# Fewer switches of the TensorE array in a head pair: regrouped full-array work, split score units and a hand order for VectorE

## The chip, the core and the metric

The kernel runs on one core of one Trainium2 chip. The metric is the device time of one execution in microseconds; the kernel before took 359.49 us (median of 3 runs, 359.22 to 360.35). Five engines work side by side, each through its own list of instructions in order: TensorE (PE; its weight loads are shown as PEld), VectorE (DVE), ScalarE (ACT), GpSimd (POOL) and SyncE (SP, which here only issues transfers). They wait for each other with semaphores. TensorE writes to PSUM[...]; VectorE and ScalarE read it.

## The reference

Two stages. Attention, for 4 batches and 8 heads of 768 positions and 64 features: keys are cut into 24 chunks of 32; each query takes the 6 chunks with the highest upper bound of its score and attends to them causally. Then a switch layer: every token goes to the one of 8 experts with the highest logit and comes back scaled by the gate.

```python
k_min, k_max = chunk minimum and maximum of k         # 24 chunks of 32 keys
ub = sum(max(q * k_min, q * k_max), features)         # upper bound per query and chunk
top_chunks = argsort(where(causal, ub, -1e9))[..., -6:]
mask = selected(top_chunks) & (pos_q >= pos_k)
attn = softmax(where(mask, (q @ k.T) / sqrt(64), -1e9)) @ v
x = attn as rows of tokens, 3072 x 512
logits = x @ w_gate; e = argmax(logits)
out = gate * (relu(x @ w1[e]) @ w2[e])                # 512 -> 1024 -> 512
```

## The kernel before: the parts concerned

A head pair is two heads of one batch, so there are 16 pairs, `i` = 0 to 15 (`b`, `hp` = batch and pair in it). The loop is pipelined over pairs: while pair `i` attends, pair `i+1` selects its chunks, pair `i+2` transposes its keys and queries, and pairs `i-1` and `i-2` turn their output into token rows. The expert stage follows the 16 pairs.

The scores of a pair are cut into 7 units of (up to) 128 keys x 384 queries x 2 heads. Each unit has a product into PSUM (`ps`), an exponential on ScalarE (`P`), a causal cut of diagonal blocks on GpSimd, a product with v into `po`, and an addition on VectorE into `acc` for the sums of the softmax. Units 0 and 1 make the output of the first 384 queries, 2 to 6 that of the others. The chosen chunks reach the scores as extra rows of the operands (`QSB` rows from 64 on, from `nsel`).

The pools, whose numbers of buffers matter:

```python
ps_m = tc.alloc_tile_pool(name="ps_m", bufs=3, space=PSUM)   # transposes, bounds, routing
ps_s = tc.alloc_tile_pool(name="ps_s", bufs=2, space=PSUM)   # scores
ps_o = tc.alloc_tile_pool(name="ps_o", bufs=1, space=PSUM)   # attention output "po"
...
ot = work.tile([128, 384], FP32, tag="ot", bufs=3)           # output, copied from po
```

Preparation of a pair (the full array is used by the transposes of 128 columns; `ub` has two 64-column halves; `mask` transposes 64 columns):

```python
def k_half(hf):                      # steps k0, k1
    ... nc.tensor.transpose(pt, k tile) x3
    nc.vector.tensor_reduce(kmx, pk, max); nc.vector.tensor_reduce(kmn, pk, min)
    nc.scalar.activation(kte[0:64, 0, ...], pt[0:64]); nc.scalar.activation(kte[0:64, 1, ...], pt[64:128])
def q_t(hf):  ... nc.tensor.transpose(pt, q tile) x3              # q0, q1
def q_e(hf):  # q0e, q1e: VectorE copies qT, ScalarE makes qA = |q| and QSB; GpSimd copies QSB later
def kse():    # VectorE, for each head: KS = kmx + kmn, KD = kmx - kmn (4 operations)
def ub():     # TensorE: KS.T @ qT + KD.T @ qA; ScalarE copies it to ubT
def select(): # TensorE transposes ubT x3; VectorE: + bias, top 8 of 24 (12 operations), nsel = below the 6th
def mask():   # TensorE transposes nsel x6; ScalarE copies both heads to QSB
```

Scores and output:

```python
def scores(i, u):
    ps = ps_s.tile([128, 2, 512], FP32, tag="s")
    for n, (kb, w, c0) in enumerate(parts):        # units 1 and 6 have two parts, 256 and 128 queries
        for hd in range(2):
            nc.tensor.matmul(pv[:, hd, :], lhsT=kte[:, hd, ts(kb, 128)], rhs=qsb[...])
    for pv, (kb, w, c0) in zip(pvs, parts):
        nc.scalar.activation(P[:, :, ds(c0, w)], pv, AF.Exp)        # one for each part
    ...                                                             # causal cut on GpSimd
def attend(i, u):
    if first: s["po"] = ps_o.tile([128, 384], FP32, tag="o")
    ... nc.tensor.matmul(po[64 * hd:64 * hd + 64, ...], lhsT=vt[...], rhs=P[...])
    if last:  nc.vector.tensor_copy(out=ot[:], in_=po[:])
    if not first: nc.vector.tensor_tensor(acc, acc, P, ALU.add)     # for each part
```

Routing rows, `router_steps`: `ud` (sums and logits by TensorE in 32-column products, copied by ScalarE), `lgp` (transposes of `ud`; VectorE: reciprocal and `lgt`), `x0`, `x1` (transposes of `ot`; VectorE scales them into `xrow`). `route_steps`, once per batch: `logits` (with the gates), `rank`, `scatter`.

The loop, with TensorE, GpSimd and SyncE in the order written and VectorE and ScalarE ordered by the scheduler:

```python
groups = [(0, 1), (2, 3), (4, 5), (6,)]
with tc.manual_schedule(engines={PE, POOL, SP}):
    with tc.manual_schedule(engines={DVE, ACT}): first_pair()
    consts_last(); load(2, "k", "q")
    run(prep, 1, "k0", "k1", "q0", "q0e", "q1", "q1e", "kse")
    for i in range(NP):
        for g in range(4):
            if g == 0:   scores(i, 2); scores(i, 3); run(rout, i - 2, "x1")
            elif g == 1: scores(i, 4); scores(i, 5); [rank of the batch before]; run(prep, i + 1, "select")
            elif g == 2: scores(i, 6); run(prep, i + 2, "k0"); run(prep, i + 1, "mask")
            else:
                run(rout, i - 1, "lgp", "x0")
                scores(i + 1, 0); scores(i + 1, 1)
                run(prep, i + 2, "k1", "q0", "q0e", "q1")
            for u in groups[g]: attend(i, u)
            if g == 3: run(prep, i + 2, "q1e", "kse")
            if g == 0: run(prep, i + 1, "ub"); flush()
            ...
            if g == 1: run(rout, i - 1, "ud")
```

Of the kernel before, what the change touches and what calls it, by code (L numbers as in the profile page):

```python
# [24 lines left out]
def kernel(  # L25
# [74 lines left out]
    KS = [buf.tile([128, 64], FP32, name=f"KS{i}") for i in range(2)]  # L100
    KD = [buf.tile([128, 64], FP32, name=f"KD{i}") for i in range(2)]
# [6 lines left out]
    def consts_first():  # L108
# [12 lines left out]
        nc.gpsimd.memset(KS[0][:], 0.0)  # L121
        nc.gpsimd.memset(KD[0][:], 0.0)
# [15 lines left out]
    def consts_last():  # L138
        nc.gpsimd.memset(KS[1][:], 0.0)
        nc.gpsimd.memset(KD[1][:], 0.0)  # L140
# [53 lines left out]
    def prep_steps(i):  # L194
        s = st[i]
        kte, qsb, ks, kd = KTE[i % 2], QSB[i % 2], KS[i % 2], KD[i % 2]
        kmx = {}

        def k_half(hf):
            if hf == 0:  # L200
                s["kmx"] = work.tile([128, NCH], FP32, tag="kmx", name="kmx")
                s["kmn"] = work.tile([128, NCH], FP32, tag="kmn", name="kmn")
            pt = ps_m.tile([128, 384], FP32, tag="m")
            for t in range(3):
                nc.tensor.transpose(pt[:, ts(t, 128)], s["k"][:, 3 * hf + t], ident_f[:])
            pk = pt[:].rearrange("p (c w) -> p c w", w=CH)
            nc.vector.tensor_reduce(s["kmx"][:, ts(hf, 12)], pk, AX.X, ALU.max)
            nc.vector.tensor_reduce(s["kmn"][:, ts(hf, 12)], pk, AX.X, ALU.min)
            nc.scalar.activation(kte[0:64, 0, ts(hf, 384)], pt[0:64, :], AF.Copy, bias=0.0, scale=0.125)
            nc.scalar.activation(kte[0:64, 1, ts(hf, 384)], pt[64:128, :], AF.Copy, bias=0.0, scale=0.125)  # L210

        def q_t(hf):
            pt = ps_m.tile([128, 384], FP32, tag="m")
            for t in range(3):
                nc.tensor.transpose(pt[:, ts(t, 128)], s["q"][:, 3 * hf + t], ident_f[:])
            s[f"qp{hf}"] = pt

        def q_e(hf):
            pt = s[f"qp{hf}"]
# [3 lines left out]
            qT, qA = s["qT"], s["qA"]  # L223
            nc.vector.tensor_copy(out=qT[:, hf], in_=pt[:])  # L224
            nc.scalar.activation(qA[:, hf], pt[:], AF.Abs)
            late.append(lambda: nc.gpsimd.tensor_copy(out=qsb[0:64, 0, ts(hf, 384)], in_=qT[0:64, hf]))  # L226
            nc.scalar.activation(qsb[0:64, 1, ts(hf, 384)], pt[64:128, :], AF.Copy)

        def kse():
            for hd in range(2):  # L230
                r = slice(64 * hd, 64 * hd + 64)
                c = slice(32 * hd, 32 * hd + NCH)
                nc.vector.tensor_tensor(ks[r, c], s["kmx"][r, :], s["kmn"][r, :], ALU.add)
                nc.vector.tensor_tensor(kd[r, c], s["kmx"][r, :], s["kmn"][r, :], ALU.subtract)

        def ub():
            pu = ps_m.tile([128, 384], FP32, tag="m")
            for w_, nm in ((ks, "qT"), (kd, "qA")):
                x_ = s[nm][:].rearrange("p a c -> p (a c)")
                for h in range(2):  # L240
                    nc.tensor.matmul(pu[64 * h:64 * h + 64, 0:320], lhsT=w_[:], rhs=x_[:, ds(128 + 320 * h, 320)],
# [4 lines left out]
        def select():  # L246
            pt = ps_m.tile([128, 3, 2, 2, 32], FP32, tag="m")
            for t in range(3):
                nc.tensor.transpose(pt[:, t], s["ubT"][:, ds(c0s[t], 128)], ident_f[:])
            ubm = work.tile([128, 3, 2, 2, NCH], FP32, tag="ubm")  # L250
# [14 lines left out]
        def mask():  # L265
            pt = ps_m.tile([64, S], BF16, tag="m")
            for hf in range(2):
                for t in range(3):
                    nc.tensor.transpose(pt[:, ds(128 + 320 * hf + c0s[t], 128)],
                                        nsel[:, t, hf].rearrange("p a n -> p (a n)"), ident_b[:])  # L270
            nc.scalar.activation(qsb[64:64 + NCH, 0, 128:S], pt[0:NCH, 128:S], AF.Copy)
            nc.scalar.activation(qsb[64:64 + NCH, 1, 128:S], pt[32:32 + NCH, 128:S], AF.Copy)

        return dict(k0=lambda: k_half(0), k1=lambda: k_half(1), q0=lambda: q_t(0),
                    q1=lambda: q_t(1), q0e=lambda: q_e(0), q1e=lambda: q_e(1), kse=kse, ub=ub, select=select, mask=mask)


# [4 lines left out]
    def scores(i, u):  # L282
        kte, qsb = KTE[i % 2], QSB[i % 2]
        qb, parts = units[u]
        ps = ps_s.tile([128, 2, 512], FP32, tag="s", name="ps")
        if u in (0, 2):
            P = work.tile([128, 2, 384], FP32, tag="Pa", bufs=4, name="Pa")
        else:
            P = work.tile([128, 2, 384], FP32, tag="Pr", bufs=4, name="Pr")
        st[i][f"P{u}"] = P  # L290
        pvs = []
        for n, (kb, w, c0) in enumerate(parts):
            if len(parts) == 1:
                pv = ps[:, :, 0:w]
            else:
                pv = ps[:, n, 0:2 * w].rearrange("p (a w) -> p a w", a=2)
            for hd in range(2):
                nc.tensor.matmul(pv[:, hd, :], lhsT=kte[:, hd, ts(kb, 128)],  # L298
                                 rhs=qsb[:, hd, ds(qb * 384 + 384 - w, w)],
                                 start=True, stop=True, skip_group_check=True)  # L300
            pvs.append(pv)
        for pv, (kb, w, c0) in zip(pvs, parts):
            nc.scalar.activation(P[:, :, ds(c0, w)], pv, AF.Exp)  # L303
        for n, (kb, w, c0) in enumerate(parts):
# [5 lines left out]
    def attend(i, u):  # L310
# [4 lines left out]
        if first:  # L315
            s["po"] = ps_o.tile([128, 384], FP32, tag="o", name="po")
        po = s["po"]
# [5 lines left out]
        if last:  # L323
            ot = work.tile([128, 384], FP32, tag="ot", bufs=3)
            nc.vector.tensor_copy(out=ot[:], in_=po[:])  # L325
            s[f"ot{qb}"] = ot
        if first:
            s[f"acc{qb}"] = P
        else:
            acc = s[f"acc{qb}"]  # L330
            for n, (kb, w, c0) in enumerate(parts):
                nc.vector.tensor_tensor(acc[:, :, 384 - w:384], acc[:, :, 384 - w:384],  # L332
                                        P[:, :, ds(c0, w)], ALU.add)

    def router_steps(i):
# [22 lines left out]
        def lgp():  # L358
            pt = ps_m.tile([128, 3, 2, 2, 32], FP32, tag="m")
            for t in range(3):  # L360
                nc.tensor.transpose(pt[:, t], s["ud"][:, ts(t, 128)], ident_f[:])
            rec = work.tile([128, 3, 2, 2, 1], FP32, tag="rec", bufs=2)
# [20 lines left out]
        def xr(hf):  # L383
            pt = ps_m.tile([128, 3, 2, 64], FP32, tag="m")
            for t in range(3):
                nc.tensor.transpose(pt[:, t].rearrange("p a d -> p (a d)"),
                                    s[f"ot{hf}"][:, ts(t, 128)], ident_f[:])
            nc.vector.tensor_tensor(
# [3 lines left out]
        return dict(ud=ud, lgp=lgp, x0=lambda: xr(0), x1=lambda: xr(1))  # L392

    def route_steps(b):
        def logits():
# [17 lines left out]
            ex = work.tile([128, 6, E], FP32, tag="ex")  # L413
            nc.scalar.activation(ex[:], sh[:], AF.Exp)
            se = work.tile([128, 6], FP32, tag="se")
            nc.vector.tensor_reduce(se[:], ex[:], AX.X, ALU.add)
            nc.vector.tensor_scalar(se[:], se[:], 1e-9, None, ALU.add)
            for hf in range(2):
# [3 lines left out]
                d = nc.vector.tensor_copy(out=xr[:, :, DM + 2:DM + 4].bitcast(I32),  # L422
                                          in_=tokid[:, b, hf, :].unsqueeze(2))
                if b < B - 1:
                    tc.keep_in_program_order(d)
            bst[b]["oh"] = oh

        def rank():
# [445 lines left out]
```

## Time and profile before

| what | before |
|---|---|
| time, median of 3 runs | 359.49 us |
| span of the profiled execution | 358.6 us |
| ScalarE exponential, 128 x 768 / 512 / 256 | 0.81 / 0.59 / 0.39 us |
| VectorE addition into `acc`, 768 / 512 / 256 | 0.95 / 0.67 / 0.46 us |
| VectorE copy `ot`, 128 x 384 | 0.55 us |
| VectorE KS / KD operation, 64 x 24 | 0.35 / 0.24 us |
| attention stage, first output product of pair 0 / of pair 15 | 21.4 / 233.6 us |

In lines of groups and of the order of time, an entry reads: start, duration, engine, line of the kernel, operation, output tile and input tile with their shapes, count; in brackets the idle time of the engine just before and what ended it. Instructions of one engine overlap by a little, so the step from start to start is shorter than the duration: a 0.81 us exponential is followed 0.71 us later by the next. What an engine is busy in a stretch does not say what that stretch waits for: that is read from the order of time and from the idle times in it.

### The profile page before, as it was taken

The page shows a single profiled execution, that of the slowest core. Times are in us where ns is not written, and L with a number is a line of the kernel's source. Part 1 is how long each engine was busy: PE and PEld are TensorE (multiplying, and loading weights), DVE is VectorE, ACT ScalarE, POOL GpSimd, SP SyncE. Part 2 cuts the span into 40 slices and gives each one's busy share as a digit, 9 for nine tenths or more (in the row PEclk, how much of TensorE's full clock was granted, in tenths as well). Part 3 has the DMA queues.
Part 4 walks back from the last instruction along what each step waited for, and adds up shares of the span by engine and source line. Part 5 has one row for each costly group of instructions (what it writes and reads, how often), then busy time and mean ns, then how long its engine had stood idle before and what let it go on. Part 6 is the DMA issues. An engine that isn't in the chain of part 4 may idle for free. (4 is left out here: it accounts for less than half of the span.)

```text
span 358.6 us, 7585 instructions
## 1 busy us (share of the span) xinstructions
PE 326.9 (91%) x2312; PEld 171.5 (48%) x2312; DVE 235.0 (66%) x815; ACT 231.2 (64%) x398; POOL 180.4 (50%) x296
## 2 busy tenths in 40 slices
PE   6679999999899999999999988998799999999990
PEld 5535455455455465554554545443344344444430
DVE  5799889889999898999988999846460000000000
ACT  2497797797687897867977967642344444445440
POOL 3075425445474453466534547575577665653331
PEclk9999999999999999999999999999999999999996
DMA  8619998999957999937989973476999999998851
GB/s 153 112 26 194 210 220 139 215 167 215 207 127 151 182 176 195 202 100 178 200 134 212 187 148 113 73 135 116 165 211 233 221 237 197 203 186 201 157 126 48
DMA packets 138215, 59.83 MB, mean 167 GB/s; under 512 B 122811, under 2 KB 131005, under 8 KB 138176
## 3 DMA queue, kind: packets, MB, share of 16 engines
q1 hardware_dynamic: 119072, 29.52, 45.4%
q0 software_dynamic: 17536, 29.42, 42.0%
q10 hardware_dynamic: 1568, 0.39, 0.6%
q8 instruction: 21, 0.34, 0.4%
q14 instruction: 18, 0.15, 0.2%
HBM read 56.14 MB, written 10.51 MB: 186 GB/s over the span
## 5 line engine op out<-in xcount | busy, mean ns | idle before, releaser
L332 DVE TENSOR_TENSOR Pa<-Pa,Pr 128x768 f32<-128x768 f32 (+2 forms) x112 | 81.6, 729 | 1.1
L307 POOL TENSOR_SCALAR_AFFINE_SELECT Pr<-Pr 128x256 f32<-128x256 f32 x80 | 33.5, 437 | 67.3 <-ACT Pr L303 66.1
L303 ACT ACTIVATE Pr<-ps 128x768 f32<-128x768 f32 (+2 forms) x112 | 65.0, 630 | 3.2 <-PE ps L298 2.9
L612 PE MATMUL py<-w_all,hT 128*128 x224 | 52.7, 379 | 2.7 <-DMA hT<-h__3653 1.9
L298 PE MATMUL ps<-QSB,KTE 128*128 128x384 bf16 (+2 forms) x288 | 50.4, 292 | 1.2 <-DVE QSB L711 0.2
L620 POOL DMA_INDIRECT out_dram<-y,ti_all x28 | 27.8, 993 | 30.2 <-ACT y L619 26.3
L298 PEld LDWEIGHTS <-KTE 128*128 128x128 bf16 x288 | 24.1, 97 | 27.3 <-issue 21.2
L612 PEld LDWEIGHTS <-hT 128*128 128x128 bf16 x224 | 21.8, 98 | 29.5 <-DMA hT<-h__3653 2.3
L619 ACT ACTIVATE y<-py,gt_all 128x512 f32<-128x512 f32 x27 | 18.6, 687 | 20.8 <-PE py L612 18.4
L454 POOL DMA_INDIRECT xs_dram<-xrow,sli x24 | 26.9, 1121 | 7.7 <-issue 5.0
L356 ACT ACTIVATE ud<-pu 128x384 f32<-128x384 f32 x16 | 7.9, 492 | 32.8 <-PE pu L353 30.7
L303 ACT ACTIVATE Pa<-ps 128x768 f32<-128x768 f32 x32 | 26.0, 812 | 3.8 <-PE ps L298 3.2
L601 PE MATMUL ph<-w_all,KTE 128*128 x120 | 28.4, 379 | 0.0
L169 POOL DMA_DIRECT2D w_all<-in_moe_w_dram x32 | 24.3, 760 | 0.0
L307 POOL TENSOR_SCALAR_AFFINE_SELECT Pa<-Pa 128x256 f32<-128x256 f32 x16 | 6.4, 398 | 35.3 <-ACT Pa L303 35.3
L601 PE MATMUL ph<-w_all,QSB 128*128 x96 | 22.7, 379 | 0.3 <-issue 0.3
L575 DVE TENSOR_TENSOR ti_all<-xgqA,inv_i 128x1 int32<-128x1 int32 x9 | 1.4, 159 | 29.6 <-DMA xgqA<-xs_dram,grow 29.6
L554 POOL DMA_INDIRECT xgqA<-xs_dram,grow x14 | 14.6, 1046 | 10.2 <-issue 3.3
L554 POOL DMA_INDIRECT xgqT<-xs_dram,grow x14 | 14.5, 1033 | 8.7 <-DVE gt_all L577 4.9
L325 DVE COPY ot<-po 128x384 f32<-128x384 f32 x32 | 17.7, 553 | 1.6 <-PE po L320 0.9
L575 DVE TENSOR_TENSOR ti_all<-xgqT,inv_i 128x1 int32<-128x1 int32 x8 | 1.3, 159 | 26.5 <-DMA xgqT<-xs_dram,grow 26.5
L226 POOL CAST QSB<-qT 64x384 bf16<-64x384 f32 x30 | 16.3, 551 | 4.1 <-DVE qT L224 2.8
(311 smaller groups left out, 665.0 us busy)
## 6 DMA issues: line engine op xcount, KB each, us to landing
w_all<-in_moe_w_dram POOLq DMA_DIRECT2D x32, 512.0 KB, 6.0
out_dram<-y,ti_all POOLq DMA_INDIRECT x28, 3.6
t__122<-in_k_dram SPq DMA_DIRECT2D x2, 192.0 KB, 3.5
t__125<-in_q_dram ACTq DMA_DIRECT2D x2, 192.0 KB, 4.0
t__128<-in_v_dram SPq DMA_DIRECT2D x2, 192.0 KB
t__196<-in_k_dram SPq DMA_DIRECT2D x2, 192.0 KB, 3.1
t__206<-in_q_dram SPq DMA_DIRECT2D x2, 192.0 KB, 3.8
t__209<-in_v_dram SPq DMA_DIRECT2D x2, 192.0 KB
```

The source lines that it names most:

```text
L169: nc.gpsimd.dma_start(out=dst, in_=src.rearrange("(c p) f -> p c f", p=128))
L298: nc.tensor.matmul(pv[:, hd, :], lhsT=kte[:, hd, ts(kb, 128)], rhs=qsb[:, hd, ds(qb * 384 + 384 - w, w)], start=True, stop=True, skip_grou ...
L303: nc.scalar.activation(P[:, :, ds(c0, w)], pv, AF.Exp)
L307: nc.gpsimd.affine_select(out=pd, in_=pd, pattern=[[0, 2], [1, 128]], compare_op=ALU.is_ge, fill=0.0, base=0, channel_multiplier=-1)
L325: nc.vector.tensor_copy(out=ot[:], in_=po[:])
L332: nc.vector.tensor_tensor(acc[:, :, 384 - w:384], acc[:, :, 384 - w:384], P[:, :, ds(c0, w)], ALU.add)
L454: d = nc.gpsimd.indirect_dma_start(out=xs_dram[:], out_offset=bass.IndirectOffsetOnAxis(ap=sli[:, u:u + 1], axis=0), in_=bst[b][f"xrow{u % ...
L554: d = nc.gpsimd.indirect_dma_start(out=xg_bufs[j % XB].bitcast(I32), out_offset=None, in_=xs_dram[:], in_offset=bass.IndirectOffsetOnAxis( ...
L601: nc.tensor.matmul(ph[:, fh, :], lhsT=xT[:, c, :], rhs=w_all[:, ds(wo + (c * F + fh * 512), 512)], start=(c == 0), stop=(c == NDC - 1), sk ...
L612: nc.tensor.matmul(py[:], lhsT=hT[:, c, :], rhs=w_all[:, ds(wo + (W1W + c * DM), DM)], start=(c == 0), stop=(c == NFC - 1))
L619: nc.scalar.activation(y[:], py[:], AF.Copy, bias=0.0, scale=fs[j]["gt"])
L620: d = nc.gpsimd.indirect_dma_start(out=out[:], out_offset=bass.IndirectOffsetOnAxis(ap=fs[j]["ti"], axis=0), in_=y[:], in_offset=None, bou ...
```

## The change

It regroups the work so that TensorE is used with all 128 columns in two places of a head pair (groups 1 and 3) instead of four, because a change between 128-column and 64-column products costs TensorE time. The scores of units 2, 3 and 6, which stand among 64-column products, are themselves split into two 64-column halves. VectorE gets the order written; every step is cut into its TensorE part and its VectorE part so that both orders can be given. The output of units 2 to 6 is copied out by ScalarE instead of VectorE. KS and KD become one tile made by three operations; units 1 and 6 have one exponential instead of two. The pools and the expert stage are as before.

```diff
-    KS = ...; KD = ...
+    KSD = [buf.tile([128, 2, 2, 32], FP32, name=f"KSD{i}") for i in range(2)]
+    bm = buf.tile([128, 2, NCH], BF16, name="bm")          # 1 for the head's own rows, else 0
...
+        def kse():
+            nc.vector.tensor_tensor(kt2[:, 0], kmx, kmn, ALU.add)
+            nc.vector.tensor_tensor(kt2[:, 1], kmx, kmn, ALU.subtract)
+            nc.vector.tensor_tensor(ksd[:, :, :, 0:NCH], kt2 (spread), bm (spread), ALU.mult)
...
-    def scores(i, u):
+    def scores(i, u, split=False):
+        n = 64 if split else 128
+        for kb, w, c0 in parts:
+            for hd in range(2):
+                for h in range(128 // n):
+                    nc.tensor.matmul(ps[ds(h * n, n), hd, ds(c0, w)], lhsT=kte[:, hd, ds(kb * 128 + h * n, n)], ...)
+        nc.scalar.activation(P[:], ps[:, :, 0:384], AF.Exp)
...
-    def attend(i, u):
+    def av(i, u):      # the products alone
+    def add(i, u):     # the additions alone
+    def o_ev(i, qb):
+        ot = work.tile([128, 384], FP32, tag="ot", bufs=3, name="ot")
+        if qb == 0:
+            nc.vector.tensor_copy(out=ot[:], in_=st[i][f"po{qb}"][:])
+        else:
+            nc.scalar.activation(ot[:], st[i][f"po{qb}"][:], AF.Copy)
...
-    with tc.manual_schedule(engines={PE, POOL, SP}):
+    with tc.manual_schedule(engines={PE, POOL, SP, DVE}):
...
                 if g == 0:
-                    scores(i, 2); scores(i, 3); run(rout, i - 2, "x1")
+                    scores(i, 2, True); scores(i, 3, True)
+                    av(i, 0); av(i, 1); o_ev(i, 0)
+                    if router: logits()
+                    add(i, 1)
+                    if router: gates()
+                    run(prep, n, "ub"); flush()                    # n = i + 1, m = i + 2
                 elif g == 1:
                     scores(i, 4); scores(i, 5)
-                    [rank]; run(prep, i + 1, "select")
+                    run(prep, n, "sel_mm"); run(rout, i - 2, "x_mm", 1); run(prep, m, "k_mm", 0)
+                    if router: rank_mm()
+                    run(prep, n, "sel_v")
+                    if router: rank_v()
+                    run(rout, i - 2, "x_v", 1); run(prep, m, "k_v", 0); run(prep, m, "k_a", 0)
+                    av(i, 2); av(i, 3); add(i, 3); run(rout, i - 1, "ud")
                 elif g == 2:
-                    scores(i, 6); run(prep, i + 2, "k0"); run(prep, i + 1, "mask")
+                    scores(i, 6, True); run(prep, n, "mask")
+                    av(i, 4); av(i, 5); add(i, 4)
                 else:
-                    run(rout, i - 1, "lgp", "x0")
+                    run(rout, i - 1, "lgp_mm"); run(rout, i - 1, "x_mm", 0)
                     scores(i + 1, 0); scores(i + 1, 1)
-                    run(prep, i + 2, "k1", "q0", "q0e", "q1")
+                    run(rout, i - 1, "lgp_v"); run(rout, i - 1, "x_v", 0)
+                    run(prep, m, "k_mm", 1); run(prep, m, "k_v", 1); run(prep, m, "k_a", 1)
+                    for hf in range(2): q_mm, q_v, q_a of m
+                    av(i, 6); o_ev(i, 1); run(prep, m, "kse")
+                    add(i, 5); add(i, 6)
```

The routing of a batch (`logits`, `gates`, `rank_mm`, `rank_v`) now stands in the second pair of the next batch, pairs 5, 9 and 13 ("router pairs"). The constants of `consts_last` (a comparison for U128, base_e, eight for tri8, on VectorE) stand before the preparation of pair 1 in the text, and VectorE now keeps that order.

## The prediction

> **What bounds the kernel now.** I read the page first, then the busy time by stretch of one head pair, then ScalarE's instructions in order of time over that pair, and last the built instruction order of both kernels with the semaphore each instruction waits for.
>
> The page's first part, and the busy time of one steady pair (after the times: PE, PEld, DVE, ACT, POOL, TensorE clock, DMA share, GB/s):
>
> ```profile
> PE 326.9 (91%) x2312; PEld 171.5 (48%) x2312; DVE 235.0 (66%) x815; ACT 231.2 (64%) x398; POOL 180.4 (50%) x296
> ...
> 115.40:129.10 13.70, 13.62 (x111) 7.48 (x110) 12.66 (x40) 11.40 (x22) 5.57 (x12) 1.00 0.99 166
> ```
>
> The shares over the span mislead: they average the attention stage and the expert stage. In a pair TensorE has no gap, VectorE is busy 92% and ScalarE 83%. The first attention-output matmul of successive pairs stands at 62.58, 76.23 and 89.89 us, a period of 13.66 us. ScalarE in one pair:
>
> ```profile
> 116.02 0.81 ACT L303 ACTIVATE Pa<-ps 128x768 f32<-128x768 f32 x1
> 116.73 0.87 ACT L303 ACTIVATE Pr<-ps 128x512 f32<-128x512 f32 x2
> 117.81 0.48 ACT L209 ACTIVATE KTE<-pt 64x384 bf16<-64x384 f32 x1 [0.21 <-DVE kmn L208]
> 118.30 0.49 ACT L210 ACTIVATE KTE<-pt 64x384 bf16<-64x384 f32 x1
> 118.81 0.49 ACT L225 ACTIVATE qA<-pt 128x384 f32<-128x384 f32 x1
> 119.32 0.49 ACT L227 ACTIVATE QSB<-pt 64x384 bf16<-64x384 f32 x1
> 119.83 0.81 ACT L303 ACTIVATE Pa<-ps 128x768 f32<-128x768 f32 x1
> 120.54 0.48 ACT L225 ACTIVATE qA<-pt 128x384 f32<-128x384 f32 x1
> 121.05 0.49 ACT L227 ACTIVATE QSB<-pt 64x384 bf16<-64x384 f32 x1
> 121.56 0.81 ACT L303 ACTIVATE Pr<-ps 128x768 f32<-128x768 f32 x1
> 122.27 0.43 ACT L244 ACTIVATE ubT<-pu 128x320 f32<-128x320 f32 x1
> 122.58 1.52 ACT L303 ACTIVATE Pr<-ps 128x768 f32<-128x768 f32 x2
> 125.97 0.49 ACT L356 ACTIVATE ud<-pu 128x384 f32<-128x384 f32 x1 [1.87 <-PE pu L353]
> 126.36 0.87 ACT L303 ACTIVATE Pr<-ps 128x512 f32<-128x512 f32 x2
> 127.25 0.69 ACT L271 ACTIVATE QSB<-pt 24x640 bf16<-24x640 bf16 x1
> 127.95 0.69 ACT L272 ACTIVATE QSB<-pt 24x640 bf16<-24x640 bf16 x1
> 128.67 0.48 ACT L209 ACTIVATE KTE<-pt 64x384 bf16<-64x384 f32 x1
> ```
>
> ScalarE has one real gap, 1.87 us, before `ud`. From `ud` on it runs without one until the exponentials of units 4 and 5. TensorE waits for it once: the second half of the 121.84 us scores starts 0.24 us late because their PSUM tile is freed only by the exponential ending at about 122.4. So the pair is a balance of full TensorE and a long in-order ScalarE run. And ScalarE does the exponential of unit 2 (119.83) between the two q halves; the attention output is copied out by VectorE at 118.23 us, so the next pair's output matmuls start at 119.32.
>
> **What the Trainium skill says.** TensorEngine Tiling (Array Packing), Key Properties: "Changing tiling mode (not just tile) drains the TensorE". The trace agrees: the start-to-start step that goes from a 128-column to a 64-column matmul is 0.202 us where it is 0.109 within the mode, and the next one has 0.05 more; going back costs 0.10 to 0.11. Same page, Restrictions: column tiling disables fast weight load; the 64-column loads of `nsel` take 109 ns against 97 for 128-column ones of `KTE`. TensorE: Matmul & The Clock Gate, the table at its top: ScalarE, VectorE and GpSimd are strict FIFO; every timeline I read is in the built order. Same page, Part 1: an idle window of some 3.4 us halves the TensorE clock; before has no such idle time in attention (clock 1.00), so no run here shows it yet.
>
> **The change part by part, TensorE.** One visit to the full array costs about 0.11 + 0.15 = 0.26 us; two fewer save 0.52 us per pair. Splitting unit 6 costs about 0.1 (the two 128-wide halves become load-bound); units 2 and 3 are 384 wide, two 64-column tiles side by side, no loss. TensorE's own work falls from 13.66, less about 0.38 of waits, to about 12.85. If nothing else moved: 0.8 us x 16, about 13 us gained.
>
> **VectorE** loses one `ot` copy (0.47) and some 0.3 to 0.6 of the KS/KD work (four ops of 0.24 to 0.35 become three); its need is about 11.8. **ScalarE** gains `ot` (0.49) and loses 0.16 twice (one exponential for units 1 and 6). Neither total is the trouble; the order is.
>
> Three things in the built order of after turn against it.
>
> 1. On ScalarE `ot` stands behind both q halves, and the exponentials of units 2 and 3 behind it. The output PSUM pool has one buffer, and the next pair's unit-0 output matmul waits for this `ot`.
> 2. On VectorE the `ot` copy of unit 1 waits for the x transposes of two pairs earlier (three `ot` buffers), which now come after the scores of units 4 and 5 and the selection transposes, not before the output matmuls.
> 3. VectorE in hand order does the constants (U128, base_e, tri8) before pair 1's reductions; they need the last iota of GpSimd.
>
> One steady pair, t = 0 at unit 0's output matmul; steps are start-to-start times of the same instructions before. TensorE: units 0, 1 at 0.65 each, bound products 4 x 0.263, switch 0.10 (2.46); scores 4, 5 0.66 (3.12); selection and x transposes 0.38 + 0.36, done in PSUM at 4.1; k transposes. The VectorE `ot` copy runs 4.15 to 4.65, so unit 2's matmuls start at 4.75 instead of 4.3; units 2, 3 1.35, switch, `ud` products 0.92 (7.1), switch, scores 6 0.4 and 0.3 to arrive: unit 6's exponential starts at 7.85. VectorE meanwhile: unit 1 adds 1.1 (5.75), selection 0.45 + 1.1 + 0.45 (7.75), xrow 0.5, k reductions 0.95 (9.2), two adds 1.8 (11.0), `rec` and `lgt` 0.65, xrow 0.5, k reductions 1.0 (13.2). ScalarE: exponential 0.71, mask 2 x 0.71 (10.0), k 2 x 0.5 (11.0), two exponentials of the next pair (12.4), wait for the k reductions (13.2), k 1.0, q 4 x 0.51 (16.25), `ot` 0.49 (16.75). Next unit 0 at 16.8. **A pair takes 16.8 us against 13.66: 3.1 more**, with TensorE idle nearly 4 us of it, mostly before unit 0.
>
> The router pairs (5, 9, 13; 15.74, 15.74 and 17.42 us now): 6 small VectorE ops for logits (1.2) and 6 for gates (0.8) come before the selection, the rank matmuls wait for the selection's PSUM tile (8.2), the rank ops (0.9) before the k reductions (12.1), and ScalarE has its k copies ahead of `ud`. The same walk gives 21.7 us: +6, +6, +5.
>
> Start: GpSimd's last iota ended at 24.03 us; constants 1 us, so pair 1's k reductions start at 25.0 where they started at 18.12. The second q transposes of pair 1 wait for them and stand before pair 0's scores 2 and 3. Unit 0 of pair 0: 21.40 becomes about 29, with TensorE perhaps at half clock after 8 us of rest: +7.5.
>
> Sum: start 7.5; pair 0 (no `ud`) 1.5; pair 1 (14.31 to 16.2) 1.9; pairs 2, 3, 4, 6, 7, 8, 11, 12 8 x 3.1 = 25; pair 10 (13.92 now) 2.9; routers 17; pair 14 (no k, q) and the expert stage, whose program is the same, 0. Together 56; I take off 4, because where several waits meet, some of my slack may be counted twice. **359.5 + 52 = 411 us.**
>
> **Rivals.** (a) The switches are what counts, and the in-order waits hide in slack: 347 us. For it: TensorE is full and every drain is visible in its steps. Against: 7.85 + 8.9 us is one closed chain, and the ScalarE part alone, unit 6's exponential to the second QSB, is 8.8 us before (112.70 to 121.54) with one exponential in it. (b) Only the ScalarE chain bites, `ot` after x and the late reductions do not: 7.4 + 8.3 = 15.7 per pair, routers +3 each, start +7: about 398. (c) VectorE in a hand order is what costs, ScalarE having slack: then only start and routers, less the drains: about 371. Against: VectorE needs 11.8 of 13.66, but `ot` on ScalarE closes the loop whatever VectorE does. (d) TensorE, idle 4 us a pair, is throttled too: 430 or more. The rests are shorter than a window except in router pairs and at the start.
>
> **Range and chances.** 0.9 us of doubt in ten plain pairs is 9 us, 2 us in three router pairs 6, the start 2; with the rivals (b) and (d) at its ends: 393 to 430. Faster needs (a), and the semaphores read against it: 0.04; same 0.02; slower 0.94.
>
> **What would show it.** Right: `po<-Pa` of TensorE waiting 2 to 3 us for ACT `ot` in every pair; an `ot` copy on VectorE that waits for PE `px`; the first `kmx` of pair 1 at about 25 us; a period near 16.8 and router pairs near 21; full-array steps in two places of a pair. Wrong: a period under 14, TensorE still without gaps, or ScalarE doing `ot` before the q halves.

## The result, and the profile after

| what | before | after |
|---|---|---|
| time, median | 359.86 us (359.22 to 360.35) | 426.33 us (425.09 to 427.24) |
| ratio after / before, 95% interval | | 1.185 (1.181 to 1.189) |
| span of the profiled execution | 358.6 us | 424.9 us |
| first output product of pair 0 | 21.40 us | 30.33 us |
| plain pair, from one first output product to the next | 13.66 us | 16.91 us |
| router pairs 5, 9, 13 | 15.74, 15.74, 17.42 us | 21.52 us each |

The change made the kernel slower by 66 us, where 52 were predicted. Where they come from, by the start times of unit 0's output product in successive pairs: the start 8.9, pair 0 3.0, pair 1 3.4, the eight plain pairs 29.5, pair 10 3.0, the router pairs 15.7, pair 14 3.6; what follows the start of pair 15 is 0.6 us shorter.

The page's first part, and the TensorE clock that was granted in 40 slices:

```profile
PE 338.8 (80%) x2440; PEld 186.0 (44%) x2440; DVE 235.8 (55%) x783; ACT 237.1 (56%) x382; POOL 188.7 (44%) x297
...
PEclk9959899998989899999999999899999999999996
```

VectorE is busy as long as before (235.8 us against 235.0), ScalarE 6 us longer (the `ot` copies) and TensorE 12, on a span 66 us longer. So the time went into waiting, and the clock row has a 5 and several 8s where before was at full clock in attention. Busy time in one steady pair (columns as for before: PE, PEld, DVE, ACT, POOL, clock, DMA share, GB/s):

```profile
245.97:262.89 16.92, 13.61 (x116) 8.05 (x117) 12.90 (x37) 11.76 (x21) 7.19 (x13) 1.00 0.99 164
```

TensorE has the 13.6 us of before, so its 12 us more over the span are not more work in a pair; they go with the clock, which was at half for 42.7 us of the span against 8.0 before. Every engine has over 3 us of rest: a pair in which no engine is the bound is bound by a chain that runs through several of them. ScalarE in that pair, in order of time, shows the chain:

```profile
253.57 0.49 ACT L368 ACTIVATE ud<-pu 128x384 f32<-128x384 f32 x1 [3.03 <-PE pu L365]
253.96 0.81 ACT L312 ACTIVATE Pr<-ps 128x768 f32<-128x768 f32 x1
254.78 1.40 ACT L285 ACTIVATE QSB<-pm 24x640 bf16<-24x640 bf16 x2
256.20 0.98 ACT L216 ACTIVATE KTE<-pk 64x384 bf16<-64x384 f32 x2
257.21 0.81 ACT L312 ACTIVATE Pa<-ps 128x768 f32<-128x768 f32 x1
...
259.28 0.98 ACT L216 ACTIVATE KTE<-pk 64x384 bf16<-64x384 f32 x2 [0.56 <-DVE kmn L211]
...
261.79 0.49 ACT L242 ACTIVATE QSB<-pq 64x384 bf16<-64x384 f32 x1
262.30 0.49 ACT L344 ACTIVATE ot<-po 128x384 f32<-128x384 f32 x1
```

From unit 6's exponential at 253.96 to the late `ot` at 262.30 there are 8.3 us with one rest of 0.56: mask, k half, two exponentials of the next pair, k half, four q operations, and only then `ot`. TensorE at both ends of the pair:

```profile
245.97 0.87 PE L329 MATMUL po<-Pa,t__2782 128*64 128x384 f32 x4 [2.56 <-issue]
...
250.68 0.87 PE L329 MATMUL po<-Pa,t__2782 128*64 128x384 f32 x4 [0.32 <-DVE ot L342]
...
262.89 0.54 PE L329 MATMUL po<-Pa,t__2985 128*64 128x384 f32 x2 [2.58 <-issue]
```

Unit 0's first product starts 0.1 us after `ot` has left the one output PSUM buffer (262.30 + 0.49), after 2.58 us of rest. The profile puts the rest down to "issue", because the wait is an instruction of its own ahead of the product; which semaphore it is has to be read from the program, where it is ScalarE's `ot`. The 0.32 us is the second wait, unit 2's product for VectorE's `ot`. That copy itself stood waiting, on an engine with nothing else to do:

```profile
250.06 0.56 DVE L342 COPY ot<-po 128x384 f32<-128x384 f32 x1 [3.40 <-PE px L403]
```

Its data were there when unit 1's products ended, some 2.5 us earlier; it waits for its SBUF buffer, which the x transposes of two pairs before still have to read. In the list of waits (engine, line, what for: total, times, longest) both appear among the longest, with the ones of the start and of the router pairs:

```profile
DVE ot L342 <- PE px L403: 51.4, 14, 5.8
...
ACT KTE L216 <- DVE kmn L211: 31.7, 18, 7.4
PE po L329 <- issue: 28.4, 11, 2.6
...
PE pr L453 <- DVE ubm L264: 11.3, 3, 3.8
...
DVE U L157 <- POOL colf L105: 7.2, 1, 7.2
```

The 7.2 us are VectorE at the start. It holds the ten constants back for GpSimd's last iota, and pair 1's reductions stand behind them:

```profile
25.10 0.29 DVE L157 TENSOR_SCALAR U<-colf,iota_p 128x128 bf16<-128x128 f32 x1 [7.21 <-POOL colf L105]
...
26.06 0.56 DVE L210 TENSOR_REDUCE kmx<-pk 128x12 f32<-128x384 f32 x1
```

Last, what the prediction had only for the start and the router pairs: stretches of half clock in the middle of attention. Two neighbouring stretches of 3.4 us around the start of pair 4 (PE busy is the first number after the length, the clock is the one before the DMA share):

```profile
94.10:97.50 3.40, 1.33 (x16) 0.71 (x13) 3.26 (x8) 3.02 (x7) 2.92 (x7) 1.00 1.12 220
97.50:100.90 3.40, 2.91 (x14) 1.83 (x16) 1.08 (x2) 1.80 (x3) 0.00 (x0) 0.51 1.25 194
```

The first holds the rest before unit 0 and has TensorE busy for 1.33 us of 3.40; in the second TensorE runs at 0.51 of its clock. Pair 4 takes 18.35 us instead of 16.91.

### The profile page after: what moved, and what is told of

It reads as the page before. It is cut to its first block, busy times and chain, and to the rows that moved or that the text cites. A ratio compares the mean times of both kernels' runs of the same rounds, so it can differ in the third digit from the quotient of the medians.

```text
span 424.9 us, 7721 instructions
## 1 busy us (share of the span) xinstructions
PE 338.8 (80%) x2440; PEld 186.0 (44%) x2440; DVE 235.8 (55%) x783; ACT 237.1 (56%) x382; POOL 188.7 (44%) x297
## 5 line engine op out<-in xcount | busy, mean ns | idle before, releaser
L316 POOL TENSOR_SCALAR_AFFINE_SELECT Pr<-Pr 128x256 f32<-128x256 f32 x80 | 44.0, 568 | 123.5 <-ACT Pr L312 123.5
L312 ACT ACTIVATE Pr<-ps 128x768 f32<-128x768 f32 x80 | 63.1, 809 | 2.2 <-DVE nsel L275 1.4
L303 PE MATMUL ps<-QSB,KTE 128*64 128x384 bf16 (+5 forms) x416 | 49.4, 295 | 2.2 <-ACT QSB L285 1.9
L216 ACT ACTIVATE KTE<-pk 64x384 bf16<-64x384 f32 x60 | 29.1, 485 | 32.3 <-DVE kmn L211 31.7
L342 DVE COPY ot<-po 128x384 f32<-128x384 f32 x16 | 8.9, 558 | 56.5 <-PE px L403 51.4
L303 PEld LDWEIGHTS <-KTE 128*64 128x64 bf16 (+1 forms) x416 | 27.4, 106 | 24.4 <-issue 18.2
L479 POOL DMA_INDIRECT xs_dram<-xrow,sli x24 | 24.2, 1008 | 22.5 <-DVE base_e L473 17.4
L644 ACT ACTIVATE y<-py,gt_all 128x512 f32<-128x512 f32 x27 | 18.5, 687 | 21.6 <-PE py L637 21.6
L253 ACT ACTIVATE ubT<-pu 128x320 f32<-128x320 f32 x16 | 7.0, 437 | 28.0 <-PE pu L249 28.0
L285 ACT ACTIVATE QSB<-pm 24x640 bf16<-24x640 bf16 x30 | 20.8, 692 | 2.0 <-PE pm L282 1.4
L210 DVE TENSOR_REDUCE kmx<-pk 128x12 f32<-128x384 f32 x32 | 17.6, 550 | 6.3 <-PE pk L205 6.3
```

The lines of the kernel that those rows point to most:

```text
L216: nc.scalar.activation(kte[0:64, hd, ts(hf, 384)], pt[64 * hd:64 * hd + 64, :], AF.Copy, bias=0.0, scale=0.125)
L285: nc.scalar.activation(qsb[64:64 + NCH, hd, 128:S], pt[32 * hd:32 * hd + NCH, 128:S], AF.Copy)
L303: nc.tensor.matmul(ps[ds(h * n, n), hd, ds(c0, w)], lhsT=kte[:, hd, ds(kb * 128 + h * n, n)], rhs=qsb[:, hd, ds(qb * 384 + 384 - w, w)], s ...
L312: nc.scalar.activation(P[:], ps[:, :, 0:384], AF.Exp)
L316: nc.gpsimd.affine_select(out=pd, in_=pd, pattern=[[0, 2], [1, 128]], compare_op=ALU.is_ge, fill=0.0, base=0, channel_multiplier=-1)
L479: d = nc.gpsimd.indirect_dma_start(out=xs_dram[:], out_offset=bass.IndirectOffsetOnAxis(ap=sli[:, u:u + 1], axis=0), in_=bst[b][f"xrow{u % ...
```

## The experiments

The theory: a loop of TensorE (unit 0's product to unit 6's exponential) and ScalarE (that exponential to the late `ot`), lengthened by VectorE's `ot` behind the x transposes; the constants at the start and the routing ahead of the selection come on top. Rivals: VectorE's hand order as such; the drains of TensorE; ScalarE's work as such. The first four runs were on a chip on which the kernel before took 364.77 us, the others on chips with 359.95 to 361.59: times are compared as ratios to the kernel before on the same chip.

| run | first product of pair 0 | plain pair | router pairs | time / before (95%) |
|---|---|---|---|---|
| before | 21.40 us | 13.66 us | 15.7 to 17.4 us | 1 |
| after | 30.33 | 16.91 | 21.5 | 1.185 (1.181 to 1.189) |
| e1 `ot` ahead of the q halves | 29.61 | 15.47 | 20.1 to 20.7 | 1.116 (1.101 to 1.130) |
| e2 `ot` on VectorE | 30.32 | 15.07 | 19.7 to 20.3 | 1.100 (1.088 to 1.112) |
| e3 x transposes early | 30.69 | 16.15 / 17.84 | 18.0 to 19.4 | 1.140 (1.128 to 1.153) |
| e4 constants late | 22.79 | 16.90 | 21.5 | 1.185 (1.171 to 1.199) |
| e5 VectorE scheduled | 22.38 | 17.04 | 17.3 to 17.9 | not given |
| e6 scores unsplit | 31.17 | 16.91 | 21.5 to 23.0 | 1.193 (1.183 to 1.203) |
| e7 unit 6 early | 30.25 | 15.53 | 20.4 to 21.2 | 1.114 (1.105 to 1.123) |
| e8 three undone | 23.35 | 14.24 | 16.5 to 17.9 | 1.045 (1.037 to 1.054) |
| e9 all moves, unit 6 early | 20.87 | 14.83 | 17.7 to 18.5 | 1.071 (1.065 to 1.076) |
| e10 the same, unsplit | 21.08 | 14.82 | 17.7 to 18.5 | 1.073 (1.068 to 1.079) |
| e11 before + `ot` on ScalarE | 23.50 | 14.51 | 16.0 to 16.2 | 1.018 (1.013 to 1.023) |
| e12 all moves, unit 6 late | 20.96 | 13.77 | 16.1 to 17.6 | 1.029 (1.023 to 1.035) |

"Plain pair" is the value that most undisturbed plain pairs have.

### e1: `ot` ahead of the q halves

```diff
                     for hf in range(2):
                         run(prep, m, "q_mm", hf)
                         run(prep, m, "q_v", hf)
-                        run(prep, m, "q_a", hf)
...
                     av(i, 6)
                     o_ev(i, 1)
+                    for hf in range(2):
+                        run(prep, m, "q_a", hf)
```

> Changed kernel, with the calls for the ScalarE halves of q moved behind the copy of the late output, so that ScalarE does ot before them; nothing else. Loop theory (the pair's period is one closed chain from unit 0's output product over unit 6's exponential to ScalarE's ot): the four q copies, 2.0 us, leave the chain, but the exponentials of units 2 and 3 then stand behind them and hold the scores of units 4 and 5 by some 0.6 us: plain period 16.9 to about 15.5, time about 406 us. VectorE theory (the hand order alone sets the period): ot is no part of the chain, no change, 426. Drain theory (the array's switches decide): no change, 426.

Measured: plain pairs of 15.47 us, 1.44 less than after, with the same instructions. The order of five ScalarE operations is worth that much; TensorE's waits ahead of output products fell from 36.3 us in 14 to 9.6 us in 17. (These are the ones that the profile puts down to "issue" and to GpSimd's `QSB` taken together: for the rest before unit 0 it gives now one, now the other.)

### e2: `ot` back on VectorE

```diff
-        if qb == 0:
-            nc.vector.tensor_copy(out=ot[:], in_=st[i][f"po{qb}"][:])
-        else:
-            nc.scalar.activation(ot[:], st[i][f"po{qb}"][:], AF.Copy)
+        nc.vector.tensor_copy(out=ot[:], in_=st[i][f"po{qb}"][:])
```

> Changed kernel, with the late output copied by VectorE again, right behind its two q copies; all else stays. Loop theory: unit 0 of the next pair can start when VectorE has done it, about 14.7 after the last one, some 0.4 us more for a ubT that is late: period about 15.1, time about 401 us. VectorE theory: VectorE gets 0.5 us more in every pair, so slower: period 17.4, time about 433 us. Drain theory: no change, 426.

Measured: 15.07 us, ratio 1.100. VectorE gets 0.47 us more a pair and the pair gets 1.84 shorter, so VectorE's amount of work is not what counts. ScalarE gets 0.49 us less here; e1, which leaves the work of both as it is, shows that the copy's place on ScalarE counts.

### e3: x transposes before units 0 and 1

```diff
                     scores(i, 3, True)
+                    run(rout, i - 2, "x_mm", 1)
+                    run(rout, i - 2, "x_v", 1)
                     av(i, 0)
...
-                    run(rout, i - 2, "x_mm", 1)
```

(and the VectorE part of the step out of group 1). ScalarE's scheduler also moved the first k half ahead of unit 6's exponential. It stays in the chain there: in the pair that starts at 166.6 us it ends at 174.7 us, just when that exponential starts, so its 1.0 us lies ahead of the exponential instead of behind the mask.

> Changed kernel, with the x transposes of two pairs earlier back in front of the output products of units 0 and 1, so that VectorE's ot copy no longer waits for them; TensorE gets a third visit to the full array. (The scheduler of ScalarE then also puts the first k copies ahead of unit 6's exponential.) Loop theory: 0.45 us at unit 2 and 0.6 us at the second k copies leave the chain: period about 16.0, routers 1.5 less, time about 412 us. VectorE theory: VectorE no longer stands for 3.4 us and is 2 us earlier everywhere: period under 15, under 400 us. Drain theory: one visit more, 0.26 us: 430 us.

Measured: every second plain pair takes 16.15 us, as expected, and every other 17.84. The long ones hold a stretch at half clock; those stretches begin at 80.8, 114.9, 149.0, 183.2, 217.3 and 251.4 us, 34.13 us apart, which is ten times 3.41 and nearly two pairs (33.99). So a rest that returns with the pair falls into the same place of the clock's windows every second time. Two of the router pairs are 18.0 and the third 19.4 instead of 21.5 us, each with such a stretch in it: VectorE's `ot` no longer stands in the way there.

### e4: the constants behind pair 1's preparation

```diff
-        nc.vector.tensor_scalar(U128[:], ...); nc.vector.tensor_copy(out=base_e[:], ...); tri8 ...
...
         prep[1]["kse"]()
+        consts_v(colf)        # the same ten operations
         flush()
```

> Changed kernel, with VectorE's constants (U128, base_e, tri8) after pair 1's preparation instead of before it. Every theory that has the start as a term of its own: unit 0 of pair 0 at about 22.3 instead of 30.3 us, time about 418 us, period unchanged at 16.9. If the start hides behind later slack (loads, for one), the first unit comes earlier but the time stays within 2 us of 426.

Measured: the start comes 7.5 us earlier, as the theory had it, and the time is that of after (ratio 1.185), as the rival had it. By the start of pair 15 only 1.2 us of the gain are left (299.3 us against 300.5). Pair 0 takes 18.45 us instead of 16.16: the earlier work meets a load that is not there yet, which is what the rival expected and which after does not wait for, and half clock follows.

```profile
29.81 0.52 PE L208 MATMUL pk<-ident_f,t__375 128*128 128x128 f32 x3 [2.71 <-DMA t__375<-in_k_dram]
```

The same wait, 2.7 to 3.5 us, is in pair 0 of e5, e8, e9 and e12. The other 4.0 us, net, went with the clock: four plain pairs (2, 6, 7, 12) and pair 10 take 18.3 to 18.5 us, and there are eleven stretches of half clock between the start of pair 0 and the end of attention, where after has seven. That the earlier start brought them is not shown. The seven microseconds were really gained and lost again elsewhere, which is why a total alone would have misled.

### e5: VectorE given back to the scheduler

```diff
-    with tc.manual_schedule(engines={PE, POOL, SP, DVE}):
-        with tc.manual_schedule(engines={ACT}): first_pair()
+    with tc.manual_schedule(engines={PE, POOL, SP}):
+        with tc.manual_schedule(engines={DVE, ACT}): first_pair()
```

> The kernel after with one thing undone: VectorE's order is given back to the scheduler; ScalarE's late ot stays behind both q halves, the x transposes and the full-array visits stay moved. Loop theory (the chain from unit 6's exponential over mask, k, q to ot on ScalarE closes the loop, whoever orders VectorE): the scheduler lets pair 1's reductions go ahead of the constants, so unit 0 of pair 0 starts near 22.5 us instead of 30.3, and a plain pair takes 16.0 to 16.9 us; 1.14 to 1.18 times the kernel before. Rival (c), VectorE's hand order is what costs: a plain pair near 13.7, 1.00 to 1.02.

The two timed executions, 404.14 and 413.03 us (1.118 and 1.142 times before), lie over 2% apart, and the profiled one is the longer, so no single ratio is given and only what repeats from pair to pair at full clock is read. There the rival falls: a plain pair takes 17.04 us, just above the range of the loop theory and not 13.7, and the list of waits has the same line as after:

```profile
PE po L329 <- issue: 28.4, 11, 2.6
```

What the hand order does cost is the start (22.38 us against 30.33) and the router pairs (17.3 to 17.9 against 21.5).

### e6: scores unsplit

```diff
-                    scores(i, 2, True)
-                    scores(i, 3, True)
+                    scores(i, 2)
+                    scores(i, 3)
...
-                    scores(i, 6, True)
+                    scores(i, 6)
```

> The kernel after with one thing undone: units 2, 3 and 6 are scored with 128-column weights again, so TensorE changes its tiling four times a pair; all orders are kept. Loop theory: TensorE has 2.6 us of rest a pair, so only what lies between unit 0's output product and unit 6's exponential counts, 0.1 to 0.3 us a pair: period 16.9 to 17.2, ratio 1.18 to 1.20. Rival, the drains count in full (my rival (a) gave 12 us to their removal): 0.8 us a pair more, period 17.7, ratio 1.21 to 1.22.

Measured: the same plain pair to 0.01 us. The two further switches of the array fall into TensorE's rest. The time's interval overlaps that of after.

### e7: unit 6's product early

```diff
                     av(i, 5)
+                    av(i, 6)
+                    o_ev(i, 1)
                     add(i, 4)
...
-                    av(i, 6)
-                    o_ev(i, 1)
```

> The kernel after with one thing moved: unit 6's output product and its ot copy stand right behind unit 5's product, ahead of the full-array visit, so that ot on ScalarE stands before the next pair's exponentials, the second k half and the q halves, and the output PSUM buffer is free early. Loop theory: the wait of unit 0's output product for ot is gone and 2.6 us of 16.9 with it; what stays is the VectorE ot copy behind the x transposes, and TensorE's own 13 us: plain period 14.2 to 15.1, ratio 1.04 to 1.11; the start (30.3 us) stays. If something else than ot holds unit 0 of the next pair: period stays over 16.

Measured: 15.53 us, outside the 14.2 to 15.1 that were expected, and a ratio of 1.114 just above. The wait for `ot` is gone (no such line in the list of waits), but ScalarE now stands 11.2 us in 15 waits before `ot`. TensorE's longest rest in a plain pair is then 0.77 us, before the bound products, for ScalarE's `qA`; what else takes the place of the old wait was seen only in e9.

### e8: the three waits undone together

The edits of e2, e3 and e4 in one kernel.

> The kernel after with all three in-order waits taken away and the rest of the change kept (two full-array visits, split scores, VectorE in hand order): late ot on VectorE behind its q copies, x transposes of two pairs earlier before units 0 and 1, VectorE's constants behind pair 1's preparation. If the three waits are the whole of the loss: start 22 to 23 us, plain period 13.5 to 14.0, router pairs 16 to 18, ratio 0.99 to 1.03. If a further cost of the change is left (clock, splits, hand order): period over 14.3 and ratio over 1.05.

Measured: 14.24 us a plain pair and 1.045, between what was expected and the limit set for "a further cost". Of the 3.25 us that after loses in a plain pair 2.67 are gone. ScalarE shows the rest:

```profile
91.58 0.81 ACT L315 ACTIVATE Pr<-ps 128x768 f32<-128x768 f32 x1
92.33 0.98 ACT L219 ACTIVATE KTE<-pk 64x384 bf16<-64x384 f32 x2
93.34 1.41 ACT L288 ACTIVATE QSB<-pm 24x640 bf16<-24x640 bf16 x2
95.16 0.81 ACT L315 ACTIVATE Pa<-ps 128x768 f32<-128x768 f32 x1 [0.41 <-PE ps L306]
```

The k half (92.33) stands between unit 6's exponential and the mask, 1.0 us on the chain to the next pair's scores; in the kernel before it stands behind the mask. It waits for VectorE's reductions of the same tile, which end with unit 6's exponential, so it misses ScalarE's rest before `ud` (2.20 us here).

### e9: all moves, with unit 6 early

The moves of e3, e4 and e7, ScalarE in hand order too, and (core of the edit):

```diff
-                    run(prep, m, "k_v", 0)
-                    run(prep, m, "k_a", 0)
+                    run(prep, m, "k_a", 0)     # ScalarE's k half ahead of the reductions, in the rest before ud
+                    run(prep, m, "k_v", 0)
...
-                if 4 * i + g in (4 * NP - 10, 4 * NP - 9, 4 * NP - 8):     # steps of the early table
+                if 4 * i + g in (4 * NP - 7, 4 * NP - 6, 4 * NP - 5):
```

> The kernel after with its two full-array visits, split scores, ScalarE ot and VectorE hand order kept, and every in-order wait that the runs have shown taken out: unit 6's output product and ot ahead of the full-array visit; x transposes of two pairs earlier before units 0 and 1; ScalarE in hand order too, with the first k half in its rest before ud and ahead of VectorE's reductions of the same tile; VectorE's late constants behind pair 1's preparation, the bias constants ahead of the first reductions, the early table's steps behind the selection of the last prepared pair. Loop theory: no ScalarE chain is longer than TensorE's own work of 12.85 us a pair, so a plain pair takes 13.0 to 13.5 us, a router pair 16 to 17, the start is 20.5 to 22.5 us; 0.97 to 1.00 times the kernel before. Rival, a cost of the two-visit order itself that no move takes away (half-clock windows, PSUM tiles): plain pairs over 14, 1.02 or more.

A plain miss: 14.83 us and 1.071, in the rival's range; that a move can take most of it away is shown only by e12. ScalarE, GpSimd and TensorE behind unit 6's exponential:

```profile
90.29 0.81 ACT L315 ACTIVATE Pr<-ps 128x768 f32<-128x768 f32 x1
```

```profile
91.18 1.61 POOL L319 TENSOR_SCALAR_AFFINE_SELECT Pr<-Pr 128x256 f32<-128x256 f32 x2 [2.27 <-ACT Pr L315]
```

```profile
92.85 0.44 PE L332 MATMUL po<-Pr,t__1037 128*64 128x128 f32 x4 [0.42 <-POOL Pr L319]
93.22 0.55 PE L376 MATMUL pl<-ident_f,ud 128*128 128x128 f32 x3
```

Unit 6's product needs the causal cut that GpSimd makes after the exponential, and the whole full-array visit, with the next pair's scores in it, now stands behind that product: 2.56 us from the exponential to the product's second part. The work of an in-order engine must not be put behind something late merely because the late thing is short.

### e10: the same, unsplit

The edit of e6 on the kernel of e9.

> The kernel of e9 with units 2, 3 and 6 scored with 128-column weights again: four full-array visits a pair instead of two, nothing else changed. Here TensorE is the bound, so the drains should show as they could not in e6: two visits less are worth 4 x 0.15 us at most, so a plain pair is 0.3 to 0.7 us longer than in e9, 5 to 10 us in all. Rival, the drain is hidden or the 64-column loads cost as much as it saves: within 2 us of e9.

The rival holds: 14.82 against 14.83 us, 386.19 against 385.49 us. As TensorE rests 1.2 us in a pair of e9, this doesn't say what the drains are worth where TensorE is full, and no run does; here and in e6, where TensorE rests, they are not to be seen.

### e11: one part alone on the kernel before

```diff
-            nc.vector.tensor_copy(out=ot[:], in_=po[:])
+            if qb == 0:
+                nc.vector.tensor_copy(out=ot[:], in_=po[:])
+            else:
+                nc.scalar.activation(ot[:], po[:], AF.Copy)
```

> The kernel before with one part of the change alone: the late ot copy on ScalarE, where its scheduler puts it behind the first q half and ahead of the second. The copy then ends near 90.9 us where VectorE ended it at 89.4 in the pair at 76 us, and unit 0 starts 1 us later: a plain pair of 14.1 to 14.7 us against 13.66, ratio 1.02 to 1.05. Rival, ScalarE has slack for it (rival c): 13.7 us and a ratio within 1 per cent of 1. If the copy alone made the loss of after: 16 us and more.

Measured: 14.51 us a plain pair, in the range; the ratio 1.018 is a little under it. (The profiled execution is the longest of the four, 368.62 us. Beside its plain pairs the start is 2.1 us later than in before and pair 1 1.7 longer, pair 13 is 1.3 and the expert stage 1.7 shorter.) So moving the copy costs 0.85 us a pair even in the old order: ScalarE had no slack at that place. And it is a quarter of what after loses: the copy's place behind the second q half and the other waits make the rest.

### e12: all moves, with unit 6 late

```diff
-                    av(i, 6)
-                    o_ev(i, 1)
                     add(i, 4)
...
+                    av(i, 6)
+                    o_ev(i, 1)
+                    for hf in range(2):
+                        run(prep, m, "q_a", hf)
```

> The kernel of e9 with unit 6's output product and ot back behind the full-array visit, as in after, but with ot ahead of both q halves on ScalarE. In e9 the visit had to wait 2.56 us from unit 6's exponential (90.29 us) over GpSimd's select to unit 6's product (92.85), and the next scores stood behind it at 93.93; with the product behind the visit they wait only for the mask, which ends 2.24 us after the exponential starts: 1.3 us less a pair. Loop theory: plain pair 13.1 to 13.6 us (e9: 14.83), router pairs 16 to 17, start 20.5 to 22, total 0.97 to 1.01 times the kernel before, so e8's remaining 0.57 us a pair was the first k half standing between unit 6's exponential and the mask. Rival, e9's extra time was not the select: plain pair over 14.3, ratio over 1.04.

Measured: 13.77 us a plain pair, 0.47 below e8 and 1.06 below e9, so both readings hold in direction, but outside the ranges, which ended at 13.6 us and 1.01. TensorE in one of these pairs:

```profile
65.98:79.75 13.77, 13.36 (x118) 7.96 (x118) 12.82 (x37) 11.47 (x21) 7.54 (x14) 1.00 1.14 201
```

It is nearly full again, 13.36 of 13.77 us. With the waits gone the regrouped work comes out 0.26 us shorter than the 13.62 of before, not the 0.8 that I had for two visits less (the x transposes, back before unit 0, make a third short visit), and the 0.4 us of rest that is left eats it. The time is 1.029 of before. (e12 differs from e8 in more than the k half, so the 0.47 us is not shown to be that alone.) The profile has 12.5 us more than that of before: 4.7 behind the start of pair 15 (eight steps of the early table stand on VectorE there, VectorE's `ot` of pair 15 stands behind them, and unit 2's product waits 2.6 us for it), 4.2 in pair 0, 1.4 in pair 4, 1.0 in the router pairs, the rest in small pieces. In pair 0 a load is the cause:

```profile
28.55 0.52 PE L208 MATMUL pk<-ident_f,t__372 128*128 128x128 f32 x3 [3.29 <-DMA t__372<-in_k_dram]
```

With two visits the first k half is transposed ahead of units 2 and 3, and not behind unit 6's scores as before, where the same wait is 0.5 us; the k tile has one buffer, its load is not there, and TensorE runs at half clock for the 3.4 us after it. No version tried beats the kernel before.

## Why the prediction was right, and where its sizes were off

**The loop: right.** Predicted period 16.8, measured 16.91, and its two halves are right too: unit 6's exponential comes 7.99 us after unit 0's first product (7.85 in the walk), the next unit 0 8.93 after that (8.9). ScalarE does `ot` behind both q halves, TensorE rests 2.56 us for it, VectorE's `ot` waits for x. e1, e2 and e3 took the waits away one at a time and got 15.47, 15.07 and 16.15 us where the walk through the order had 15.5, 15.1 and 16.0. TensorE's own work, which the period does not rest on, was put too low: 12.85 us, where 13.61 are busy, so that its rest is 3.3 us and not nearly 4.

**The router pairs: right.** 21.7 predicted, 21.52 measured. (From 17.42 to 21.7 are 4.3 us, not the 5 of the sum, so the three routers come to 16.2 and not 17; 15.7 measured.) The rank products wait for VectorE's `ubm` 3.8 us in each, as the step had it. e5 shows that VectorE's hand order is needed for it (17.3), e3 that the x wait is needed too (18.0 to 19.4).

**The start: right in its cause, 1.4 us short.** e4 and e5 bring it back to 22.8 and 22.4 us. I had the first reduction at 25.0; it came at 26.06, because GpSimd's last iota ends at 25.06 us in after and not at 24.03 as before.

**Rivals.** (a) falls: the drains are not to be seen in e6 or e10. (b), ScalarE's chain alone, would have given 15.7 us: e3 shows that the x order adds 0.76. (c) holds for the start and the router pairs alone, as e5 shows. (d), a throttled TensorE, was set aside with "The rests are shorter than a window except in router pairs and at the start", and that step was wrong outside the router pairs. Seven stretches of half clock lie between pair 1 and pair 14. Three follow rests of 3.8 us in the router pairs, which the sentence had excepted; the other four (in pairs 1, 4, 6 and 14) come with rests of no more than 2.6 us. The term for the plain pairs was 25 and measured 29.5: 0.15 us in each of eight, 1.4 in pair 4, 1.7 in pair 6 and 0.3 in pair 8, the last without such a stretch of its own and not explained.

**Other terms.** Pairs 0 and 1 were given 1.5 and 1.9 us and took 3.0 and 3.4: e1 and e2, which change nothing but the place of `ot`, bring pair 0 to 14.3 and 13.9 us and pair 1 to 14.7 and 14.6, so the `ot` chain bites there as well, and I had counted it short; but pair 1 of after also holds a half-clock stretch (46.3 us) that e1 and e2 lack, so for pair 1 the two are not told apart. Pair 14 was set at 0 and took 3.6. It has no k and q, but it has the x order. After has a stretch of half clock in it (285.3 us). In e1, whose edit does not touch this pair, it takes 15.06 us without such a stretch, 1.0 less than after; in e3, without a stretch and without the x order, 13.19, 1.9 less again and 0.6 over before. So about 1.9 of the 3.6 are the x order, which I had left out, 1.0 goes with the stretch, and the rest is open. The 4 us taken off for slack counted twice were not there.

The sum: 52 + 1.4 (start) + 3.0 (pairs 0 and 1) + 4.5 (plain pairs) + 0.1 (pair 10) - 1.3 (router pairs) + 3.6 (pair 14) + 4 - 0.6 (experts) = 66.7, against 66.3 in the spans.

**The clock rule.** The Trainium skill, TensorE: Matmul & The Clock Gate, Part 1, has the half clock come "after ≥1 idle window (~3.4µs)" and calls the window free-running. The grid of 3.41 us and the length agree with the trace; the idle window does not: the window before pair 4's stretch, shown above, has TensorE busy for 1.33 of 3.40 us. The measurement decides, and with it the rest of 2.6 us was long enough.

## What to carry to other kernels

Before moving an operation to an engine with idle time, write out what stands ahead of it there in program order and what waits for its result: a copy that frees a single PSUM buffer belongs ahead of everything that only prepares the next round. A hand order fixes every such place at once, also those that a scheduler had quietly kept right (constants behind the first reductions, routing behind the selection), so walk each engine's new order once for each kind of iteration, the first and the last too. And when a chain leaves TensorE resting in every round, add the clock to the estimate: a rest shorter than the window was enough. A gain at the start can be lost again later, here to a load that was not there yet and to the clock, so read the time from stage to stage.

## What the runs showed of the hardware

- Half clock needs no idle window. The half-clock stretches of a trace begin on a grid of 3.413 us. In the traces of all fourteen kernels, every window of that grid at full clock in which TensorE was busy for 1.42 us or less was followed by one at half clock, and none with more than 1.84 us was (e3); between 1.44 and 1.84 both occur. A window that was itself at half clock was followed by another with up to 2.82 us busy (e5).
- Stretches and pairs beat against each other: e3 had one every 34.13 us, every second pair. The grid lies differently in every profile: counted from the first instruction it begins anywhere from 0.18 us (e10) to 2.58 us (e11).
- A causal cut of GpSimd (128 x 256) took no more than 0.41 us in e9 where no VectorE addition overlapped it, and up to 1.12 us where one did. Unit 6's two cuts took 1.61 us in e9 beside additions, 1.51 us beside them in e12 (74.52 us), and 0.76 us in another pair of e12 (89.53 us), where VectorE had just ended.
